# A convolution by blocked transforms, with its inverses taken from the last block to the first, its four-term product summed during the forward transforms, and three gate steps behind the last inverse

## Chip, cores and metric

The kernel runs on one core of one Trainium2 chip. The metric is the device time of one launch in microseconds (us), the median of several runs. One launch computes the forward pass and all gradients.

## The reference, cut to what matters

```python
xn = _layernorm(x)                                  # L=2048 rows, D=576 columns
P  = jnp.exp(logdA[:, :, None] * l)                 # l = 0..L-1, N=128 modes
K  = jnp.einsum("dn,dnl,dn->dl", Cc, P, dB).real    # one kernel of length L per column
y  = irfft(rfft(xn, 2L) * rfft(K, 2L))[:L] + xn * Dskip
h  = _silu(xn @ w1) * (xn @ w3)                     # F=4608
out_0 = x + y * _silu(h @ w2)
out_1..out_12 = gradients of out_0 for the inputs, with grad_out
...
```

What follows the forward pass (the backward of the feed-forward net, of the convolution and of the kernel K) is not touched by the change.

## The kernel before, in words

The program is written as calls with a wished time (`self.at(us)`); a scheduler puts each engine's instructions in an order by these times and by the dependences, and the engines then run their lists strictly in that order, each instruction waiting for its inputs. `issue_after(x)` pins an instruction behind another. DMAs are issued from SP's list or POOL's list, so a DMA that has to wait holds everything behind it in that list.

Three streams of work overlap up to about 620 us:

- **Kernel-making** (`ssm_kernel`, `kgen_chunk`, `kgen_sum`): K is made in 36 chunks of 16 columns. For each chunk ch SP loads the table E_l (L666, issued two chunks ahead in the program), DVE negates one half of it into the other (the negate, L691), PE makes phases (et_ps, L711), ACT turns them into sines (cs_k, L713), DVE makes the products p_k (L719), q_k (L725), t_k (L732) and v_k (L736), and two chunks later PE sums v_k·q_k into kps (L749), which DVE or ACT copies into KT (L757). q_k stays in DRAM for the backward.
- **Gate steps** (`ffn_hidden`): 72 steps, numbered 0 to 71, of two row tiles each. A step is 16 matmuls of 128x512 into pgu (L1076) and 4 of 64 rows (L1084), two s_t (L1088) and two gu_t (L1089) on ACT, one h_t (L1092) on DVE, a store of h_t to H_dram on SP (L1095) and a store of gu_t to GUF_dram on POOL (L1097). `gate_mark` names for each step an earlier matmul of the convolution (`self.marks`) behind which the step's first matmul is pinned; 51 of the steps go with kernel-making, 21 with the convolution.
- **Convolution** (`ssm_conv`, `conv_half`): the columns are done in two halves h of 288, each with NB=4 blocks of 512 rows. Forward: for each block b PE makes the transform of K (L866, 32 matmuls into et_ps), ACT copies it out (kraw, L869, 8 instructions), DVE makes the variants k2, kz (L907 to L909, L959 to L963), and ACT scales kraw by signs (L965) for the next block. The transforms U of xn lie in DRAM. For output block m the product V = sum over i of K_i·U_(m-i) has m+1 terms: the first costs DVE one L917, L923, L925 and L926, a further one also L920 and L921. PE inverts V (L901, 16 matmuls), ACT copies (ev, L990), DVE adds and subtracts (s_t, L992, L993), POOL stores to S_dram (L994). Before the change all four forward blocks of a half come first, then m = 0, 1, 2, 3 with one to four terms, so the longest product stands last.

`ffn_output` then makes h·w2 for 16 row tiles. Slices of h come transposed from H_dram (hcA, hcB, hcC, L1726, on SP), the first 16 groups of w2 lie in w2a, the other 20 in w2g (ten loads on POOL, L1145, each of two groups). Tiles 0 and 1 first take the 32 matmuls with w2a each, then the 40 with w2g (L1170). The S_dram rows of a tile are loaded by POOL as s_t (L1162), x and grad_out as x_t (L1160) and go_t (L1161). Tiles 0 to 3 belong to block m=0.

Of the kernel before, what the change touches and what calls it, by code (L numbers as in the profile page):

```python
# [100 lines left out]
class K:  # L101
# [542 lines left out]
    def ssm_kernel(self, T0, TK, ps, ps1):  # L644
# [8 lines left out]
        with self.pool(name="kg_l", bufs=2) as lp, \  # L653
# [24 lines left out]
            for ch in range(NCH):  # L678
                yield T0 + TK * ch
                self.at(T0 + TK * ch)  # L680
                if ch in (20, 24):
                    self.dft_kernel_matrices(dp, (ch - 20) // 4)
                if ch % GE == 0:
                    LT_ = ahead if ch else load_lhs(0)
                elif ch % GE == 2 and ch + GE < NCH:
                    ahead = load_lhs(ch - 2 + GE)
                for c in range(3) if ch == 0 else (ch + 2,):
                    if c < NCH:
                        load_E(c)
                E, el = Es.pop(ch), self.kg_load  # L690
                nc.vector.tensor_scalar(out=E[:, 0:HW_], in0=E[:, HW_:2 * HW_], scalar1=-1.0, scalar2=None, op0=ALU.mult)  # L691
# [237 lines left out]
    def ssm_conv(self, T0, TC, ps, ps1):  # L929
        with self.pool(name="c_u", bufs=1) as up, \  # L930
# [6 lines left out]
            for h in range(2):  # L937
                self.conv_half(h, T0 + TC * h * 92, TC, kp, up, rp, ypool, tp, spool, epool, ps)

    def conv_half(self, h, T0, TC, kp, up, rp, ypool, tp, spool, epool, ps):  # L940
# [5 lines left out]
        K2, Kz, U = [], [], []  # L946
        prev = None
        fl = lambda t_: t_.rearrange("p q k d -> p q (k d)")
        self.at(T0)
        nc.vector.tensor_tensor(out=self.KT[0:1, 0, cs], in0=self.KT[0:1, 0, cs], in1=self.skip_row[:, cs], op=ALU.add)  # L950
        for b in range(NB):
            self.at(T0 + TC * 4.5 * b)
# [20 lines left out]
            Kz.append(kz)  # L973
            if h == 0 and b == NB - 1:
                with self.tc.issue_after(self.tails[-1].ins):
                    nc.gpsimd.dma_start(out=self.odd["grad_out"][:], in_=self.turned(self.aps["grad_out"].flatten_outer_dims()))
        for m in range(NB):
            self.at(T0 + TC * (18, 28, 43, 65)[m])
            u = up.tile([P, 2, 2, KT, HW], BF16, name=f"u_{m}")
            nc.sync.dma_start(out=u[:].rearrange("p q r k d -> p q (r k d)"),  # L980
                              in_=self.UH_dram[2 * h:2 * h + 2, m].rearrange("q p r k d -> p q (r k d)"))
            U.append(u)
            V = ypool.tile([P, 2, 2, KT, HW], BF16, name="V")
            for i in range(m + 1):
                self.cmul_acc(V, K2[i], Kz[i], U[m - i], tp, i == 0, False)
# [21 lines left out]
    def gate_time(self, n):  # L1007
# [3 lines left out]
        return self.KG[0] + 2 + self.KG[1] * 36 * min(i / self.GK, 1) + 7.0 * max(i - self.GK, 0)  # L1011

    def gate_mark(self, n):
# [3 lines left out]
        h, k = divmod(i - self.GK, 11)  # L1017
        return 36 + 8 * h + ((-1, 0, 1, 1, 2, 3, 3, 4, 5, 5, 6), (-1, 0, 1, 2, 3, 3, 4, 5, 5, 6))[h][k]
# [82 lines left out]
    def ffn_output(self, T0, TB):  # L1101
# [9 lines left out]
        with ExitStack() as es:  # L1111
# [3 lines left out]
            hpc, epc, ip4, gap6, hp, wpool, ipx2 = op("hc"), op("epc"), op("st", 3), op("gap6"), op("h"), op("w"), op("in2x")  # L1115
# [17 lines left out]
            turns = [[(f, f + HB, s0 + f // HB) for f in range(0, FE, HB)] + [(FE, FT, s1)] for (s0, s1) in ((42, 66), (57, 67))]  # L1133
            turns.append([(0, FT // 2, 71), (FT // 2, FT, 71)])
            w2a = self.ktp.tile([P, F0, D], BF16, name="w2a", tag="KT")
            for fi in range(0, FT, GRP):
# [899 lines left out]
def kernel(  # L2036
# [35 lines left out]
    with k.ctx:  # L2072
# [8 lines left out]
        with k.pool(name="xT", bufs=1) as xp, k.pool(name="kg_sel", bufs=1) as selp, \  # L2081
# [6 lines left out]
            k.ssm = k.ssm_forward(*k.KG, 0.83)  # L2088
# [42 lines left out]
```

## Time and profile before

| what | value |
|---|---|
| median of 3 runs (lowest, highest) | 1809.8 us (1797.02, 1814.61) |
| the profiled execution, its span | 1795.53 us, 1793.8 us |
| mean granted TensorE clock | 0.977 |
| busy over the span: PE, DVE, ACT, POOL | 91%, 76%, 50%, 19% |
| PE busy in 100 to 400 us (kernel-making with gate steps) | 274.18 of 300 us |
| PE busy in 550 to 600 us (last inverse, first products with w2) | 18.79 of 50 us |
| DMA share in these two stretches | 0.92, 0.99 |

A row of the timeline has the start, the busy time, the engine, the line, the operation with output and inputs, and how many instructions of that kind the row holds; brackets at its end give the idle time of the engine just ahead of it and what ended that. A row of the waits has the engine and line that waited, what for, the time in total, how often, and the longest. "DMA share" is the mean busy share of the 16 DMA engines, and a sum over overlapping packets, so it can pass 1.

### The profile page before, as it was taken

To read this page: it belongs to the slowest core of one execution; us is meant where nothing else is said; L and a number is where in the kernel's file an instruction comes from. 1 tells how busy PE (TensorE), PEld (TensorE's weight loads), DVE (VectorE), ACT (ScalarE), POOL (GpSimd) and SP (SyncE) were. 2 spreads that over 40 slices of the span, in tenths; PEclk is the share of its full clock that TensorE was granted. 3 is DMA by queue.
4 is the path that set the end of the run, shared out by engine and by line. 5 is a ranking of instruction groups with operands and counts; after the bars stand their busy time and mean duration, and the time that the engine had idled before them with its cause. 6 is when DMAs were issued, how large, how long until landed. Compare 5 with 4: busy or idle time off the path is not lost. (4 is left out here: it accounts for less than half of the span.)

```text
span 1793.8 us, 34839 instructions
## 1 busy us (share of the span) xinstructions
PE 1634.4 (91%) x13765; PEld 1196.3 (67%) x13765; DVE 1359.8 (76%) x2221; ACT 894.0 (50%) x1509; POOL 332.6 (19%) x536
## 2 busy tenths in 40 slices
PE   5889997999994699999999999999999998999997
PEld 2444443445442477788888888888788876778876
DVE  7667767778985355697786978659999974978665
ACT  4778786888672011576765756646454510001001
POOL 3101111111223111111111011111111144131132
PEclk9999999999998799999999999999999999999999
DMA  7879998888789989877587685679999899999991
GB/s 209 274 252 357 328 328 301 295 318 281 247 222 215 187 194 206 231 180 191 173 226 220 183 224 162 184 213 208 254 258 237 208 251 238 235 240 211 212 233 46
DMA packets 632441, 414.02 MB, mean 231 GB/s; under 512 B 427558, under 2 KB 575766, under 8 KB 627670
## 3 DMA queue, kind: packets, MB, share of 16 engines
q1 hardware_dynamic: 585228, 284.79, 64.9%
q0 software_dynamic: 32928, 114.91, 19.8%
q10 hardware_dynamic: 14122, 12.10, 2.5%
q8 instruction: 108, 1.77, 0.4%
q14 instruction: 55, 0.45, 0.1%
HBM read 130.88 MB, written 191.94 MB: 180 GB/s over the span
## 5 line engine op out<-in xcount | busy, mean ns | idle before, releaser
L1076 PE MATMUL pgu<-wmB_w,xnT 128*128 128x512 bf16 x1152 | 281.4, 384 | 5.9 <-ACT gu_t L1089 5.5
L1915 PEld LDWEIGHTS <-acts 128*128 128x128 bf16 x2304 | 225.6, 99 | 62.6 <-DMA acts<-GU_dram 3.3
L1864 PEld LDWEIGHTS <-xn_bf 128*128 128x128 bf16 x2304 | 224.1, 98 | 43.3 <-issue 17.2
L1449 DVE TENSOR_TENSOR pr_q<-et_ps,pz 128x1024 f32<-128x1024 f32 x144 | 175.9, 1222 | 29.1 <-PE et_ps L1444 20.6
L1076 PEld LDWEIGHTS <-xnT 128*128 128x128 bf16 x1152 | 108.5, 99 | 125.0 <-issue 27.2
L1915 PE MATMUL px<-wT,acts 128*128 128x288 bf16 x1472 | 191.1, 288 | 0.0
L1452 DVE TENSOR_REDUCE S_all<-pr_q 128x32 f32<-128x1024 f32 x144 | 175.2, 1217 | 3.2
L1803 PE MATMUL ph<-w2T,goT 128*128 128x256 bf16 x1440 | 172.0, 273 | 3.2 <-ACT gh L1806 3.2
L1803 PEld LDWEIGHTS <-goT 128*128 128x128 bf16 x1440 | 139.1, 98 | 21.6 <-issue 5.6
L1844 PE MATMUL pgw<-go_o,h_n 128*128 128x288 bf16 x1152 | 148.6, 286 | 0.3 <-DVE h_n L1778 0.2
L1089 ACT CAST gu_t<-pgu 128x1024 bf16<-128x1024 f32 x144 | 147.6, 1025 | 0.1
L1864 PE MATMUL pgw<-gu_n,xn_bf 128*128 128x256 bf16 x1152 | 134.5, 272 | 10.0 <-ACT gw L1848 5.9
L1097 POOL DMA_DIRECT2D GUF_dram<-gu_t x72 | 65.3, 907 | 364.4 <-ACT gu_t L1089 348.5
L1864 PE MATMUL pgw<-gg_n,xn_bf 128*128 128x256 bf16 x1152 | 130.4, 272 | 2.2 <-ACT gw L1866 2.0
L1844 PEld LDWEIGHTS <-h_n 128*128 128x128 bf16 x1152 | 112.2, 98 | 29.5 <-issue 1.8
L1088 ACT ACTIVATE s_t<-pgu 128x512 bf16<-128x512 f32 x144 | 87.9, 611 | 77.7 <-PE pgu L1076 48.2
L1866 ACT CAST gw<-pgw 128x256 bf16<-128x256 f32 x144 | 52.3, 374 | 142.0 <-PE pgw L1864 141.9
L1915 PE MATMUL px<-wA,acts 128*128 128x288 bf16 x832 | 110.7, 289 | 4.4 <-DMA acts<-GU_dram 2.7
L1806 ACT CAST gh<-ph 128x512 bf16<-128x512 f32 x144 | 81.2, 600 | 57.8 <-PE ph L1803 54.4
L1982 ACT ACTIVATE go<-gx 128x576 bf16<-128x576 f32 x15 | 10.2, 683 | 193.9 <-DVE gx L1963 146.8
L1849 POOL DMA_DIRECT2D out_dram<-gw x36 | 20.2, 560 | 335.3 <-ACT gw L1848 230.6
L713 ACT ACTIVATE cs_k<-et_ps 128x512 bf16<-128x512 int16 x144 | 75.6, 625 | 0.0
(329 smaller groups left out, 2999.2 us busy)
## 6 DMA issues: line engine op xcount, KB each, us to landing
GUF_dram<-gu_t POOLq DMA_DIRECT2D x72, 512.0 KB, 5.7
H_dram<-h_t SPq DMA_DIRECT2D x72, 256.0 KB, 3.7
Q_dram<-q_k SPq DMA_DIRECT2D x36, 512.0 KB, 4.2
gg_n<-GUF_dram POOLq DMA_DIRECT2D x18, 1024.0 KB, 6.4
h_n<-GUF_dram POOLq DMA_DIRECT2D x18, 1024.0 KB, 8.7
GG_dram<-gg_n SPq DMA_DIRECT2D x36, 512.0 KB, 10.8
GU_dram<-gu_n SPq DMA_DIRECT2D x36, 512.0 KB, 5.1
E_dram<-E_k SPq DMA_DIRECT2D x54, 256.0 KB, 2.3
```

The costliest lines, as they stand in the source:

```text
L713: self.sin_last = nc.scalar.activation(out=CS[:, :, o:o + 256], in_=pt[:].bitcast(I16)[:, :, 0::2], func=ACT.Sin, scale=6.283184 / 2 ** 16)
L1076: ins = nc.tensor.matmul(pt, lhsT=xnT[:, c, ts], rhs=wm[w][:, c, :], start=(q == 0 and c == 0), stop=(q == 1 and c == nfull - 1))
L1088: nc.scalar.activation(out=s_t[:, :, q, :], in_=pg.rearrange("p (g f) -> p g f", g=ng), func=ACT.Silu)
L1089: nc.scalar.copy(out=gu_t[:, :, :, q, :], in_=pgu[:].rearrange("p k (g f) -> p k g f", g=ng))
L1097: self.u_stores[step] = nc.gpsimd.dma_start(out=self.GUF_dram[fb * ng:(fb + 1) * ng, :, :, i0:i0 + NT, :].rearrange("g p k t f -> p k g (t ...
L1449: nc.vector.tensor_tensor(out=pr[:].rearrange("p r k e -> p r (k e)"), in0=T[x][:].rearrange("p k z d a -> p (k z d a)")[:, None].to_broad ...
L1452: nc.vector.tensor_reduce(out=self.S_all[:, :, d0:d0 + 4], in_=pr[:].rearrange("p r k (d a) -> p (r k) d a", d=4), op=ALU.add, axis=AX.X)
L1803: self.pe_last = nc.tensor.matmul(ph[j][:, k, :].rearrange("p (a f) -> p a f", f=P), lhsT=lw, rhs=rh, start=(n == 0), stop=(n == nfull))
L1806: self.sc(lambda: nc.scalar.copy(out=gh[:, j], in_=ph[j][:]))
L1844: self.pe_last = nc.tensor.matmul(pgw[pi_][:, 0:pw], lhsT=hn[:, tt, fl * P:(fl + 1) * P], rhs=go_o[:, tt, po:po + pw], start=(tt == 0), st ...
L1864: self.pe_last = nc.tensor.matmul(pw_[:, 0:FG], lhsT=self.xn_bf[:, tt, c * P:(c + 1) * P], rhs=nat[:, tt, :], start=(tt == 0), stop=(tt == ...
L1915: self.pe_last = nc.tensor.matmul(px[pi_][:, 0:pw], lhsT=acts[i][:, ai, fi, :], rhs=w[:, po:po + pw], start=(n == 0), stop=(n == len(steps ...
```

## The change

Five edits go together.

- The negate of chunk ch is pinned behind the last v_k made (that of chunk ch-1).
- In `conv_half` all four U loads move ahead of the forward blocks; V of the last block (m=3) is summed one product per forward block; the inverses then run m = 3, 2, 1, 0 with new wished times; the forward blocks have a wished distance of 8 in place of 4.5, and the second half starts at 70 in place of 92 (in units TC, now 1 and no more 0.83).
- Gate steps behind kernel-making have a wished distance of 7.4 (was 7.0) and a new table of marks: one mark for each step, so that steps 69, 70 and 71 stand behind the last inverse.
- In `ffn_output` the transposes of H (`turns`) are pinned behind later steps, and two pools change places.
- The w2g loads are pinned behind the GUF stores of steps 69 to 71, where they were pinned behind those of steps 61 to 70.

```diff
@@ ssm_kernel
-                nc.vector.tensor_scalar(out=E[:, 0:HW_], in0=E[:, HW_:2 * HW_], scalar1=-1.0, scalar2=None, op0=ALU.mult)
+                with self.tc.issue_after(self.v_last.ins) if ch else nullcontext():
+                    nc.vector.tensor_scalar(out=E[:, 0:HW_], in0=E[:, HW_:2 * HW_], scalar1=-1.0, scalar2=None, op0=ALU.mult)
@@ ssm_conv
-                self.conv_half(h, T0 + TC * h * 92, TC, kp, up, rp, ypool, tp, spool, epool, ps)
+                self.conv_half(h, T0 + TC * h * 70, TC, kp, up, rp, ypool, tp, spool, epool, ps)
@@ conv_half
+        self.at(T0 - 10)
+        for m in range(NB - 1, -1, -1):
+            U[m] = up.tile([P, 2, 2, KT, HW], BF16, name=f"u_{m}")
+            nc.sync.dma_start(out=U[m][:].rearrange("p q r k d -> p q (r k d)"),
+                              in_=self.UH_dram[2 * h:2 * h + 2, m].rearrange("q p r k d -> p q (r k d)"))
...
-            self.at(T0 + TC * 4.5 * b)
+            self.at(T0 + TC * 8 * b)
...
+            if b == 0:
+                V = ypool.tile([P, 2, 2, KT, HW], BF16, name="V")
+            self.cmul_acc(V, k2, kz, U[NB - 1 - b], tp, b == 0, False)
...
-        for m in range(NB):
-            self.at(T0 + TC * (18, 28, 43, 65)[m])
-            u = up.tile([P, 2, 2, KT, HW], BF16, name=f"u_{m}")
-            nc.sync.dma_start(out=u[:].rearrange("p q r k d -> p q (r k d)"),
-                              in_=self.UH_dram[2 * h:2 * h + 2, m].rearrange("q p r k d -> p q (r k d)"))
-            U.append(u)
-            V = ypool.tile([P, 2, 2, KT, HW], BF16, name="V")
-            for i in range(m + 1):
-                self.cmul_acc(V, K2[i], Kz[i], U[m - i], tp, i == 0, False)
+        for m in range(NB - 1, -1, -1):
+            self.at(T0 + TC * (64, 56, 48, 36)[m])
+            if m < NB - 1:
+                V = ypool.tile([P, 2, 2, KT, HW], BF16, name="V")
+                for i in range(m + 1):
+                    self.cmul_acc(V, K2[i], Kz[i], U[m - i], tp, i == 0, False)
@@ ffn_output
-                        with self.tc.issue_after(self.u_stores[61 + (fi - F0 + j) // 2].ins):
+                        with self.tc.issue_after(self.u_stores[69 + (fi - F0 + 4) // 12].ins):
```

**DVE in kernel-making**, at chunk 21. The number behind a name tells the tile: E_l_3239 is the table from which q_k_3454 and p_k_3455 are made, E_l_3434 and E_l_3558 are those of chunks 23 and 24. Before:

```order
L691 TENSOR_SCALAR E_l_3434<-E_l_3434 128x512
L691 TENSOR_SCALAR E_l_3558<-E_l_3558 128x512
L725 TENSOR_TENSOR q_k_3454<-cs_k_3437,E_l_3239 128x2x16x32 x2
L719 TENSOR_TENSOR p_k_3455<-cs_k_3437,E_l_3239 128x2x4x128
L732 TENSOR_TENSOR t_k_3461<-p_k_3455,WT_1157 128x1024 x2
L736 TENSOR_TENSOR v_k_3464<-t_k_3461 128x1024
```

and with the change:

```order
L737 TENSOR_TENSOR v_k_3379<-t_k_3376 128x1024
L1098 TENSOR_TENSOR h_t_3404<-s_t_3403,gu_t_3402 128x2x2x256
L692 TENSOR_SCALAR E_l_3239<-E_l_3239 128x512
L758 CAST KT_1296<-kps_3466 64x16x8 x2
L726 TENSOR_TENSOR q_k_3454<-cs_k_3437,E_l_3239 128x2x16x32 x2
L720 TENSOR_TENSOR p_k_3455<-cs_k_3437,E_l_3239 128x2x4x128
L733 TENSOR_TENSOR t_k_3461<-p_k_3455,WT_1157 128x1024 x2
```

Before, the negates of chunks 23 and 24 stand ahead of this chunk's q_k, and its own negate stood 30 rows earlier, some two chunks ahead. With the change its own negate stands right behind the v_k of the chunk before and two rows ahead of its q_k, and no table of a later chunk is touched ahead of it.

**ACT in the second half's forward blocks** (kraw is the copied transform, s_t and gu_t the gate steps' instructions). Before:

```order
L965 ACTIVATE kraw<-kraw,sgn 128x2304
L1088 ACTIVATE s_t<-pgu 128x2x256
L1089 CAST gu_t<-pgu 128x4x256
L1088 ACTIVATE s_t<-pgu 128x2x256
L1089 CAST gu_t<-pgu 128x4x256
L869 ACTIVATE kraw<-et_ps,hrowM 128x2x144 x2
L869 ACTIVATE kraw<-et_ps 128x2x144 x6
L965 ACTIVATE kraw<-kraw,sgn 128x2304
L869 ACTIVATE kraw<-et_ps,hrowM 128x2x144 x2
L869 ACTIVATE kraw<-et_ps 128x2x144
L1088 ACTIVATE s_t<-pgu 128x2x256
L869 ACTIVATE kraw<-et_ps 128x2x144 x2
```

and with the change:

```order
L971 ACTIVATE kraw<-kraw,sgn 128x2304
L1094 ACTIVATE s_t<-pgu 128x2x256
L1095 CAST gu_t<-pgu 128x4x256
L1094 ACTIVATE s_t<-pgu 128x2x256
L1095 CAST gu_t<-pgu 128x4x256
L870 ACTIVATE kraw<-et_ps,hrowM 128x2x144 x2
L870 ACTIVATE kraw<-et_ps 128x2x144 x6
L971 ACTIVATE kraw<-kraw,sgn 128x2304
L1094 ACTIVATE s_t<-pgu 128x2x256
```

Before, the copies of the third block are mixed with the gate step's instructions, and the sign scaling is followed by the next block's copies at once. With the change every block has the sign scaling, then a whole gate step, then the eight copies of the next block.

**POOL behind the last inverse** (s_t_6705, s_t_6754 and s_t_6911 are the S_dram rows of tiles 0, 1 and 2). Before:

```order
L1162 DMA s_t_6754<-S_dram 128x576
L994 DMA S_dram<-s_t 128x2x288
L1160 DMA x_t<-in_A_u_dram 128x576
L994 DMA S_dram<-s_t 128x2x288
L1161 DMA go_t<-in_grad_out_dram 128x576
L1160 DMA x_t<-in_A_u_dram 128x576
L1161 DMA go_t<-in_grad_out_dram 128x576
L1162 DMA s_t_6911<-S_dram 128x576
L1145 DMA w2g_6678<-in_B_w_dram 128x2x576 x2
L1145 DMA w2g_6681<-in_B_w_dram 128x2x576 x2
L1145 DMA w2g_6684<-in_B_w_dram 128x2x576 x2
L1145 DMA w2g_6687<-in_B_w_dram 128x2x576 x2
```

and with the change:

```order
L1000 DMA S_dram<-s_t 128x2x288 x2
L1167 DMA x_t<-in_A_u_dram 128x576
L1169 DMA s_t_6705<-S_dram 128x576
L1169 DMA s_t_6754<-S_dram 128x576
L1169 DMA s_t_6911<-S_dram 128x576
L1103 DMA GUF_dram<-gu_t 256x2x512
L1152 DMA w2g_6678<-in_B_w_dram 128x2x576 x2
L1152 DMA w2g_6681<-in_B_w_dram 128x2x576 x2
L1103 DMA GUF_dram<-gu_t 256x2x512
L1152 DMA w2g_6684<-in_B_w_dram 128x2x576 x2
L1152 DMA w2g_6687<-in_B_w_dram 128x2x576 x2
```

Before, the rows of tiles 0 and 1 are loaded ahead of the last two S_dram stores, and the ten w2g loads follow together. With the change the loads for all three tiles stand behind the last stores, the first four w2g loads behind the GUF store of step 69, and the other six behind that of step 70; the store of step 71 (not shown) follows them.

More of the change, by code (lines that the diff above doesn't have):

```diff
@@ L1010, in gate_time @@
         i = n - self.LEAD
-        return self.KG[0] + 2 + self.KG[1] * 36 * min(i / self.GK, 1) + 7.0 * max(i - self.GK, 0)
+        return self.KG[0] + 2 + self.KG[1] * 36 * min(i / self.GK, 1) + 7.4 * max(i - self.GK, 0)
     def gate_mark(self, n):
@@ L1016, in gate_mark @@
             return i * 36 // self.GK - 1
[L1017 to L1018 removed]
+        i -= self.GK
+        return 35 + i if i < 5 else 36 + (4, 4, 5, 6, 7, 8, 9, 10, 11, 12, 12, 13, 14, 15, 15, 15)[i - 5]
     def ffn_hidden(self, wp, gup):
```

13 lines of the change are left out of this document (7 added, 6 removed).

## The prediction

> **What bounds the kernel now.** I read the busy shares first, then a table by stage, then the waits of the two stages that the change touches, then the timeline at the longest idle times of PE. The table's columns are the stretch, its length, busy time of PE, weight loads, DVE, ACT and POOL, the granted clock, the DMA share and GB/s.
>
> ```profile
> PE 1634.4 (91%) x13765; PEld 1196.3 (67%) x13765; DVE 1359.8 (76%) x2221; ACT 894.0 (50%) x1509; POOL 332.6 (19%) x536
> 100.00:400.00 300.00, 274.18 (x1879) 132.23 (x1879) 218.18 (x423) 237.34 (x399) 47.41 (x53) 0.97 0.92 313
> 411.40:566.40 155.00, 130.21 (x771) 66.73 (x770) 133.61 (x185) 101.14 (x162) 36.02 (x44) 0.96 0.81 243
> 620.00:700.00 80.00, 79.80 (x647) 62.65 (x648) 46.15 (x68) 11.13 (x24) 13.25 (x25) 0.98 0.81 192
> ```
>
> PE is the bound, and from 620 us on it has hardly an idle moment (79.80 of 80), so what the program gains or loses before then passes through to the end. Ahead of it two stages leave PE idle: 25.8 us in kernel-making (300 - 274.18), 24.8 us in the convolution (155 - 130.21), where DVE is as busy as PE. A row of the waits of 90 to 406 us:
>
> ```profile
> DVE E_l L691 <- DMA E_l<-E_dram: 52.5, 24, 6.5
> ```
>
> DVE stood 24 times at the negate for a table that had not landed, up to 6.5 us. At the end of the convolution the waits name other causes, whose rows stand further down: PE stood 15 us for the longest product and then twice for w2g.
>
> **The change part by part.** *The negate.* Five of these waits reach PE. First the three longest of them on DVE, then the rows of PE behind all five, with the eight matmuls at 302.74 as a measure:
>
> ```profile
> 266.58 0.29 DVE L691 TENSOR_SCALAR E_l<-E_l 128x512 bf16<-128x512 bf16 x1 [6.48 <-DMA E_l<-E_dram]
> 307.37 0.29 DVE L691 TENSOR_SCALAR E_l<-E_l 128x512 bf16<-128x512 bf16 x1 [6.22 <-DMA E_l<-E_dram]
> 366.10 0.29 DVE L691 TENSOR_SCALAR E_l<-E_l 128x512 bf16<-128x512 bf16 x1 [5.02 <-DMA E_l<-E_dram]
> ...
> 198.84 0.63 PE L749 MATMUL kps<-v_k,q_k 128*128 128x64 bf16 x16 [2.86 <-DVE KT L757]
> 270.40 0.63 PE L749 MATMUL kps<-v_k,q_k 128*128 128x64 bf16 x16 [2.11 <-DVE KT L757]
> 270.86 2.95 PE L1076 MATMUL pgu<-wmB_w,xnT 128*128 128x512 bf16 x8
> 302.74 1.89 PE L1076 MATMUL pgu<-wmB_w,xnT 128*128 128x512 bf16 x8
> 313.17 0.58 PE L711 MATMUL et_ps<-SEL,lhs_t 128*128 128x256 bf16 x2 [5.62 <-ACT cs_k L713]
> 313.55 3.06 PE L1076 MATMUL pgu<-wmB_w,xnT 128*128 128x512 bf16 x8
> 332.62 0.75 PE L749 MATMUL kps<-v_k,q_k 128*128 128x64 bf16 x16 [2.04 <-DVE KT L757]
> 333.84 2.71 PE L1076 MATMUL pgu<-wmB_w,xnT 128*128 128x512 bf16 x6
> 367.36 0.63 PE L749 MATMUL kps<-v_k,q_k 128*128 128x64 bf16 x16 [1.06 <-DVE KT L757]
> ```
>
> The gaps sum to 2.86 + 2.11 + 5.62 + 2.04 + 1.06 = 13.7 us. Behind three of them the next matmuls run slowly: eight take 2.95 and 3.06 where eight take 1.89 elsewhere, and six take 2.71 where 1.42 (six eighths of 1.89) would do, together 1.06 + 1.17 + 1.29 = 3.5 us. So 17.2 us is the upper bound of these five. The Trainium skill's page "TensorE: Matmul & The Clock Gate", Part 1, says that the array falls to half its clock only after an idle window of about 3.4 us; by that rule only the gap of 5.62 would bring slow matmuls, and the bound would be 13.7 + 1.2 = 14.9. The trace does not bear it out that strictly: eight matmuls took 2.95 us behind a gap of 2.11.
>
> Will the wait be gone? The order shows the negate of a chunk behind the v_k of the chunk before, two or so chunks later than it stood. A load lands within 9.2 us of its issue:
>
> ```profile
> DMA to landing us min/median/max: 3.3/5.1/9.2
> ...
> L691 DVE TENSOR_SCALAR E_l<-E_l x36: 284/294/295, 109.3 to 380.2; 128x512 bf16<-128x512 bf16 x36
> ```
>
> The negates from 109.3 to 380.2 give a chunk each 7.7 us (271 / 35), so two chunks are 15 us of cover, more than the longest landing; SP's list has the loads where they were. What the negate costs itself (0.29) does not change. What is late next? The other small waits (25.8 - 13.7 = 12.1 us) stay, and the DMA share of 0.92 would rise to 0.97 if the stage shrank by 15 us. I take 15 of the 17.2, and for the range 3 (if most of it turns into other waits) to 19 (if small idle times go too).
>
> *The convolution's own work* is the same: 20 products, 8 transforms, 8 inverses; only the order moves. The rows for DVE (busy, mean ns), the first transform and its scaling, two products in a row, and three sign scalings of the second half:
>
> ```profile
> L921 DVE TENSOR_TENSOR V<-V,cm_t 128x2304 bf16<-128x2304 bf16 x12 | 16.1, 1343 | 0.0
> L925 DVE TENSOR_TENSOR V<-V,cm_t 128x1152 bf16<-128x1152 bf16 x20 | 14.9, 747 | 0.1
> ...
> 406.43 0.65 PE L866 MATMUL et_ps<-KT,dC 128*128 128x288 bf16 x4
> 414.15 2.22 ACT L965 ACTIVATE kraw<-kraw,sgn 128x2304 bf16<-128x2304 bf16 x1
> ...
> 486.80 2.21 ACT L965 ACTIVATE kraw<-kraw,sgn 128x2304 bf16<-128x2304 bf16 x1 [0.90 <-DVE kz L960]
> ...
> 487.21 1.28 DVE L917 TENSOR_TENSOR V<-k,u 128x2304 bf16<-128x2304 bf16 x1
> 488.42 1.33 DVE L923 TENSOR_TENSOR cm_t<-u,kz 128x2304 bf16<-128x2304 bf16 x1
> ...
> 496.63 2.22 ACT L965 ACTIVATE kraw<-kraw,sgn 128x2304 bf16<-128x2304 bf16 x1 [1.31 <-DVE kz L963]
> 504.19 2.23 ACT L965 ACTIVATE kraw<-kraw,sgn 128x2304 bf16<-128x2304 bf16 x1
> ...
> L1092 DVE TENSOR_TENSOR h_t<-s_t,gu_t 128x1024 bf16<-128x1024 bf16 x22 | 15.0, 680 | 13.8 <-DMA H_dram<-h_t 13.5
> L992 DVE TENSOR_TENSOR s_t<-ev,et_ps 128x288 bf16<-128x288 f32 x16 | 7.0, 438 | 2.5 <-ACT ev L990 2.2 <-issue 0.2
> ```
>
> A first term is two full instructions (like L921) and two halves (like L925), 2 x 1.34 + 2 x 0.75 = 4.2 us; a further term is three full ones and two halves, 5.5. Instructions overlap by some 0.1 each (488.42 starts 1.21 behind 487.21, which takes 1.28), so I use 3.9 and 5.2. The new order chains, on ACT, the sign scaling, a whole gate step and the copies of the next block. The one block that went so before took 496.63 - 486.80 = 9.8 us, the mixed one 504.19 - 496.63 = 7.6. A half is then: first scaling 7.7 us after its first transform matmul (414.15 - 406.43), three times 9.8, and 7 for the last block's variants and term; then the products with three, two and one terms, 3 x 3.9 + 3 x 5.2 = 27, with four h_t (0.7) and eight additions (0.44) some 6 more in all. First half: 406.4 + 7.7 + 29.4 + 7 + 33 = 483.5. The second half's first transforms stand on PE behind the last inverse (2.2) and a gate step (16 matmuls at 302.74's rate and their tails, 4.2), so its first scaling comes at 483.5 + 14 = 497.5, and the chain ends at 497.5 + 29.4 + 7 + 33 = 567, the inverse at 569. Before, the last inverse ended at 565.80 + 3.42 = 569.2 (row below). So the stage ends where it did, with DVE waiting some 2.6 us in each block (9.8 less 7.2 of variants, term and h_t) in place of 13.5 us for H_dram. Bounds: a pitch of 7.6 makes it 6 x 2.2 = 13 earlier, 11 makes it 7 later.
>
> *Three gate steps behind the last inverse and the w2g loads.* Rows of before:
>
> ```profile
> 565.80 3.42 PE L901 MATMUL et_ps<-V,cT 128*128 128x288 bf16 x16 [15.03 <-DVE V L925]
> 570.44 0.72 POOL L994 DMA_DIRECT2D S_dram<-s_t  x1
> 572.98 4.08 PE L1170 MATMUL po<-w2a,hcB 128*128 128x288 bf16 x32
> 579.97 5.63 POOL L1145 DMA_DIRECT2D w2g<-in_B_w_dram  x8 [3.98 <-DMA x_t<-in_A_u_dram]
> 582.73 2.08 PE L1170 MATMUL po<-w2g,hcA 128*128 128x288 bf16 x8 [5.66 <-DMA w2g<-in_B_w_dram]
> 595.32 5.78 PE L1170 MATMUL po<-w2g,hcA 128*128 128x288 bf16 x28 [10.52 <-DMA w2g<-in_B_w_dram]
> 601.81 5.06 PE L1170 MATMUL po<-w2g,hcB 128*128 128x288 bf16 x40
> w2g<-in_B_w_dram POOLq DMA_DIRECT2D x10, 288.0 KB, 15.7
> S_dram<-s_t POOLq DMA_DIRECT2D x16, 144.0 KB, 4.9
> ```
>
> PE gets three steps of 4.2 that stood earlier before, and the two w2a blocks of 4.08 as before: 569 + 12.6 + 8.2 = 590 for the first w2g product. On POOL the last S_dram store is issued at about 570, and the three s_t loads behind it need it landed, 4.9 us by the median: 575; then the first four w2g loads, and the last six behind the store of step 70, near 583, held as before by older POOL DMAs (3.98) and issued over some 4 us: 587 to 590. With 15.7 us to landing the last arrive at 603 to 606, and 5.7 us of products follow (0.65 of tile 0, 5.06 of tile 1): 608 to 611, against 606.87 before. If the loads land in half that time because the ring is emptier, PE alone sets the end: 590 + 10.5 = 600. So this part is worth -7 to +5; I take 0. The page "DMA: Bandwidth & Descriptors", section "Anatomy of one DMA", of the Trainium skill has about 2.0 us fixed and bytes over 436 GB/s, by which 288 KB would land in 2.7 us and the end would be the 600; the measured 15.7, at a DMA share near 1, says that here the queue and not the transfer sets it.
>
> **Sum:** -15 + 0 + 0 = -15 against the profiled execution of 1795.5 (span 1793.8 and 1.7 around it): 1780.5. The median of the runs shown is 1809.8, 0.8% above that execution, so the forecast in its terms is 1794.8.
>
> **The rivals.** *(a) The convolution gains too.* If ACT's chain runs at 7.6 a block, since the gate step's copies no longer wait behind DVE, the last inverse comes 13 us earlier and w2g with it: -28, 1781.8. For it: DVE has 155 - 133.6 = 21 us to spare there, and the three steps cover w2g's landing. Against it: the chain of copies is in ACT's list now, word by word.
>
> *(b) Slower: the blocks wait for PE as well.* ACT's list has a gate step between scaling and copies; if that step's matmuls stand on PE behind the block's transform and are not done when ACT comes, a block takes 9.8 + 4.2 = 14.0. Six such intervals cost 25: -15 + 25 = +10, 1820. It decides from a pitch of 12.3 us on (6 x 2.5 = 15). For it: PE's marks now pin one step to each block. Against it: PE holds two pgu buffers, so a step can run ahead.
>
> *(c) The negate's wait only moves.* If the load is late because the DMA engines are full, q_k waits where the negate did: kernel-making gains 3, 1807. For it: DMA share 0.92. Against it: the wait was for tables two to three chunks ahead of their use.
>
> **How the numbers follow.** Forecast 0.47 (1794.8, its own range 1785 to 1802), (a) 0.20, (b) 0.14, (c) 0.19. The range of 8 in 10 reaches from below (a) to between (c) and (b): 1771 to 1815. A measurement of this kernel tells about 1% (18 us) from no change. Faster by more needs -18: nearly all of (a), and four in ten of the forecast's, 0.39. Slower by more needs +18, the upper part of (b) and the spread of the runs: 0.11. The same: 0.50.
>
> **What would show it.** Right: no wait of the negate for E_l beyond a few us, 52.5 before; PE busy some 274 of 285 where it was 300; the first transform near 391 in place of 406; sign scalings 9.8 apart; last inverse ending 163 us after the first transform, as before; first w2g product waiting less than 5.66 and 10.52, and the last of tile 1 200 us after the first transform. Wrong: a new wait of q_k for E_l or of PE for cs_k with 10 us or more; scalings over 12 apart; a stage behind 620 that gets longer.

## The result and the profile after

| | before | changed |
|---|---|---|
| median (lowest to highest, 20 runs each) | 1807.78 us (1787.31 to 1830.5) | 1790.7 us (1779.1 to 1807.54) |
| ratio to before, 95% interval | | 0.9932 (0.9904 to 0.996) |
| span of the profiled execution, granted clock | 1793.8 us, 0.977 | 1777.3 us, 0.983 |

The kernel became faster by 0.7%, some 12 us (0.0068 x 1807.78), where 15 were forecast; the ratio rests on the undisturbed runs, so it is a little nearer to 1 than that of the medians. In the changed file all lines stand a few further down: the negate is L692, the transforms L867, the inverses L902, the sign scaling L971, the products with w2 L1177, the transposes of h L1733.

Four landmarks on PE split the time: the first forward transform, the end of the last inverse, the end of row tile 1's products with w2, and the start of tile 4's. The second figure is the distance from the first transform.

| landmark | before | changed |
|---|---|---|
| first transform starts | 406.43 | 385.96 |
| last inverse ends | 569.2 (162.8) | 554.8 (168.8) |
| tile 1's products end | 606.87 (200.4) | 589.64 (203.7) |
| tile 4's products start | 630.94 (224.5) | 617.45 (231.5) |
| rest of the span behind that | 1162.9 | 1159.9 |

The start of tile 4's products in the old kernel, and in the changed one the end of the last inverse, of tile 1's products and the start of tile 4's (that row is cut off by the end of its view):

```profile
630.94 4.08 PE L1170 MATMUL po<-w2a,hcB 128*128 128x288 bf16 x32
```

```profile
554.13 0.65 PE L902 MATMUL et_ps<-V,cT 128*128 128x288 bf16 x4 [0.42 <-ACT ev L996]
...
584.58 5.06 PE L1177 MATMUL po<-w2g,hcB 128*128 128x288 bf16 x40
...
617.45 2.74 PE L1177 MATMUL po<-w2a,hcB 128*128 128x288 bf16 x21
```

In these two profiles kernel-making gave 20.5 us, and the convolution with the first row tiles took 7.0 of them back. The stage table of the old kernel, from 100 us to the first transform and from there to the end of tile 1's products (columns as in the prediction):

```profile
100.00:406.43 306.43, 280.47 (x1927) 135.36 (x1926) 222.72 (x432) 242.35 (x408) 48.32 (x54) 0.97 0.92 313
406.43:606.87 200.44, 159.24 (x968) 87.55 (x967) 143.33 (x204) 108.12 (x175) 49.35 (x66) 0.92 0.89 237
```

and of the changed one:

```profile
100.00:385.96 285.96, 272.64 (x1926) 132.30 (x1926) 224.20 (x433) 241.63 (x408) 48.35 (x54) 0.99 0.97 336
385.96:589.64 203.68, 167.70 (x967) 90.53 (x966) 141.55 (x200) 109.17 (x175) 48.55 (x64) 0.92 0.73 217
```

In the first stage PE's idle time fell from 26.0 to 13.3 us (length less busy) and its busy time, for the same 1926 matmuls, from 280.5 to 272.6: 12.6 us of waiting and 7.8 of slower matmuls are gone. In the second the idle time fell too, from 41.2 to 36.0, but the same matmuls took 8.5 us longer.

The waits of the convolution and of the first row tiles in the changed kernel (engine and line, what for, total, times, longest):

```profile
PE et_ps L902 <- DVE V L926: 23.6, 6, 6.2
...
PE et_ps L867 <- ACT kraw L870: 7.3, 7, 2.0
...
PE po L1177 <- DMA hcA<-H_dram: 6.1, 1, 6.1
```

and from its timeline on PE the first transform, the inverses that waited, and the first products with w2g:

```profile
385.96 0.65 PE L867 MATMUL et_ps<-KT,dC 128*128 128x288 bf16 x4
...
430.60 2.97 PE L902 MATMUL et_ps<-V,cT 128*128 128x288 bf16 x16 [1.98 <-DVE V L926]
448.68 4.00 PE L902 MATMUL et_ps<-V,cT 128*128 128x288 bf16 x16 [5.90 <-DVE V L926]
460.06 3.45 PE L902 MATMUL et_ps<-V,cT 128*128 128x288 bf16 x16 [3.29 <-DVE V L926]
...
514.67 3.45 PE L902 MATMUL et_ps<-V,cT 128*128 128x288 bf16 x16 [3.28 <-DVE V L926]
532.51 4.00 PE L902 MATMUL et_ps<-V,cT 128*128 128x288 bf16 x16 [6.20 <-DVE V L926]
544.33 3.70 PE L902 MATMUL et_ps<-V,cT 128*128 128x288 bf16 x16 [2.99 <-DVE V L926]
...
574.75 2.12 PE L1177 MATMUL po<-w2g,hcA 128*128 128x288 bf16 x16
578.95 0.65 PE L1177 MATMUL po<-w2g,hcA 128*128 128x288 bf16 x4 [2.08 <-DMA w2g<-in_B_w_dram]
...
606.77 5.44 PE L1177 MATMUL po<-w2a,hcA 128*128 128x288 bf16 x32 [6.12 <-DMA hcA<-H_dram]
```

Where PE waited four times for a product, 18.9 us in all and 15.03 of it for the longest, it now waits six times, 2.0 to 6.2 us each and 23.6 in all, and each of the six waits is followed by slow matmuls: the 16 of such an inverse take 3.0 to 4.0 us, while twelve inverse matmuls that did not wait took 1.63 (467.44 in this timeline), so 16 take 2.2. The granted clock was 0.50 in the slow stretch from 448.70 to 452.50 and 1.00 from 467.44 to 469.00. The w2g waits shrank from 16.2 to 4.0 us in total. What is new is the wait for tile 3's transpose, 6.12 where it was 3.60.

### The profile page after: what moved, and what is told of

Read it like the earlier page. It is cut to its first block, busy times and chain, and to the rows that moved or that the text cites. A ratio compares the mean times of both kernels' runs of the same rounds, so it can differ in the third digit from the quotient of the medians.

```text
span 1777.3 us, 34850 instructions
## 1 busy us (share of the span) xinstructions
PE 1632.5 (92%) x13765; PEld 1195.1 (67%) x13765; DVE 1361.8 (77%) x2221; ACT 893.2 (50%) x1509; POOL 332.9 (19%) x536
## 5 line engine op out<-in xcount | busy, mean ns | idle before, releaser
L1098 DVE TENSOR_TENSOR h_t<-s_t,gu_t 128x1024 bf16<-128x1024 bf16 x72 | 49.6, 689 | 59.3 <-ACT gu_t L1095 57.5
```

## The experiments

Theory A: the moved negate brings the whole gain and more, by taking a wait out of DVE's list; the other edits together cost a few microseconds. Rival R: the convolution's new order brings a good part. Beside the ratios (to the old kernel, same chip, 95% interval) stand the landmarks of one profiled execution each. The rest of the span behind tile 4's start ran from 1159.6 to 1168.6 us over the profiles whose code there is alike, so that a span alone tells differences of under 9 us badly. The landmarks spread less, but they spread too: e3 and e10 below are the same kernel, and their first transforms start at 389.16 and 385.43, tile 4's products 217.0 and 223.3 us behind that. A difference of a few microseconds between two profiles is no more than a hint.

### The negate alone, and all the rest alone

```diff
# e1: the kernel before, with the negate's pin only
+                with self.tc.issue_after(self.v_last.ins) if ch else nullcontext():
+                    nc.vector.tensor_scalar(out=E[:, 0:HW_], in0=E[:, HW_:2 * HW_], scalar1=-1.0, scalar2=None, op0=ALU.mult)
# e2: the changed kernel, without the negate's pin
-                with self.tc.issue_after(self.v_last.ins) if ch else nullcontext():
-                    nc.vector.tensor_scalar(...)
+                nc.vector.tensor_scalar(...)
```

> The kernel before with only the negate of the table E_l pinned behind the v_k of the chunk before; convolution, gate marks, transposes and w2g loads as before. Theory A (the moved negate brings more than the whole gain, the other edits give a few us back): no wait of DVE for E_l, the first transform starts near 386 us instead of 406 (as in the changed kernel), and this kernel ends 17 to 21 us before the old one, ratio 0.988 to 0.991, some 3 to 7 us faster than the changed kernel. Rival R (the convolution's new order brings a good part): 8 to 12 us faster than before, ratio 0.993 to 0.996, slower than the changed kernel.

> The changed kernel with the negate put back to where it was; all other edits stay. Theory A: the first transform is back near 406 us, DVE waits some 50 us for E_l again, and the kernel is 2 to 7 us slower than before, ratio 1.001 to 1.004. Rival R: 3 to 8 us faster than before, ratio 0.996 to 0.998.

Measured: e1 0.9894 (0.985 to 0.9937), span 1778.4; e2 1.0043 (1.0009 to 1.0078), span 1812.9. First transform and start of tile 4's products in e1:

```profile
384.63 0.65 PE L867 MATMUL et_ps<-KT,dC 128*128 128x288 bf16 x4
...
611.42 4.08 PE L1171 MATMUL po<-w2a,hcB 128*128 128x288 bf16 x32
```

and in e2, with the wait of DVE that is back (waits of 90 to 406 us):

```profile
405.98 0.65 PE L866 MATMUL et_ps<-KT,dC 128*128 128x288 bf16 x4
...
645.75 4.08 PE L1176 MATMUL po<-w2a,hcB 128*128 128x288 bf16 x32
```

```profile
DVE E_l L691 <- DMA E_l<-E_dram: 53.4, 24, 6.0
```

Theory A holds and R falls: the negate alone moves the first transform by 21.8 us, and the other edits alone make the kernel slower than before, with an interval clear of 1 (tile 4 starts 239.8 us after the first transform, before 224.5). The product of both ratios, 0.9894 x 1.0043 = 0.9937, is the changed kernel's 0.9932 within the errors. That the negate alone beats the changed kernel is likely by these numbers but not settled by this run: the intervals overlap. One thing in e1 was not foreseen: its convolution stage is longer than before, though its order is the old one. The last inverse ends 170.5 us after the first transform (162.8 before, 168.8 in the changed kernel), and tile 4 starts at 226.8 (before 224.5), with DVE waiting 19.7 us for H_dram instead of 13.5.

### The negate on POOL

```diff
-                nc.vector.tensor_scalar(out=E[:, 0:HW_], ...)
+                nc.gpsimd.tensor_scalar(out=E[:, 0:HW_], ...)
```

> The kernel before with the negate of E_l done by POOL instead of DVE, at the same wished place; nothing else changed. The wait for the table's load is still there, but now POOL stands in it. Theory A (DVE standing in its list for a table needed two or three chunks later is what delayed PE): DVE no longer waits, the first transform starts at 384 to 390 us, as with the pinned negate. Rival (the pin helped by giving DVE another order, or the tables themselves are late for q_k): the first transform stays beyond 398 us, and q_k waits for POOL's negate.

> The kernel before with the negate on POOL, the same kernel as in the earlier look, now timed in five rounds since its two runs were the fastest so far. Theory A (it takes the same stall off DVE as the pin does): ratio 0.986 to 0.991, like the pinned negate alone (0.9894). If freeing DVE of the negate brings more than the pin: 0.980 to 0.985.

Measured: 0.9821 (0.9735 to 0.9908) for e3, over two runs, and 0.9877 (0.9833 to 0.992) for e10, over six; first transform at 389.16 and 385.43. The wait did not go away, it changed engines (the group in e3, then the waits in e10):

```profile
L691 POOL TENSOR_SCALAR E_l<-E_l 128x512 bf16<-128x512 bf16 x36 | 58.9, 1638 | 142.8 <-DMA E_l<-E_dram 115.7 <-DVE h_t L1092 10.3 <-DVE p_k L719 7.4
```

```profile
POOL E_l L691 <- DMA E_l<-E_dram: 108.4, 23, 26.0
```

POOL stands 108 us for the tables, twice what DVE did, and takes 1.6 to 1.7 us for each negate instead of 0.29, and still the first transform comes as early as with the pin. So neither the table's lateness nor DVE's own work was the cost, but DVE's standing in its list with q_k, v_k and the copies to KT queued behind. This bears out theory A against its rival, by a way that keeps the negate at its old wished place. The ratio of e10 lies within what was expected for "the same as the pin".

### The stalls put back

```diff
+                for _ in range({12: 2, 21: 4, 26: 4, 28: 1, 33: 3}.get(ch, 0)):     # e12: {12: 5, 17: 5, 22: 5, 27: 5, 32: 5}
+                    with self.tc.issue_after(stall.ins):
+                        stall = nc.vector.scalar_tensor_tensor(out=E[:, HW_:], in0=E[:, HW_:], scalar=1.0, in1=E[:, HW_:], op0=ALU.mult, op1=ALU.max)
```

> The changed kernel with five stalls of DVE put back by work instead of by DMA: behind the v_k of chunks 11, 20, 25, 27 and 32 DVE multiplies the table by one, 2, 4, 4, 1 and 3 times, some 1.6 us each, 22 us in all, about what the five waits lasted that reached PE in the kernel before. The output does not change. Theory A (these stalls, and the slow matmuls behind the gaps that they make, are the 20 us): the first transform moves from 386 to 396 to 406 us, with gaps of 1 to 5 us on PE and matmuls above 0.3 us behind them. Rival (DVE has slack of 70 us there, and it was the loads' DMA traffic that slowed PE): the first transform stays below 391 us.

> The changed kernel with five equal stalls of DVE by work: ahead of the negates of chunks 12, 17, 22, 27 and 32 DVE multiplies the table by one five times, 1.75 us each, 8.8 us a stall and 44 us in all. The output does not change. The earlier kernel with stalls of up to 7 us left gaps of at most 1.7 us on PE and no slow matmuls behind them; in the kernel before, gaps of 2.0 to 5.6 us were each followed by eight matmuls or so that took 1.1 to 1.2 us too long. Theory A (a gap of about 2 us or more is enough for slow matmuls, about 1.2 us for each gap whatever its length): gaps of 2 to 4 us, 1.0 to 1.3 us of slow matmuls behind each of at least three of them, first transform at 402 to 412 us. Rival (only gaps above 3.4 us are followed by slow matmuls, and what was slow in the kernel before was slow for another reason, such as DMA traffic): no slow matmuls behind the gaps of 2 to 3.4 us.

Measured: e6 0.9965 (0.9925 to 1.0004), first transform at 396.94, 11.0 us later than in the changed kernel for 14 x 1.75 = 24.5 us of added DVE work. e12 1.0007 (0.9947 to 1.0067), first transform at 405.70, 19.7 later for 25 x 1.75 = 43.8 us. By its ratio the whole gain of the change is lost in e12. The exchange is the same as for the old wait: 11.0 / 24.5 = 0.45, 19.7 / 43.8 = 0.45, and in the old kernel 20.5 / 52.5 = 0.39. So time that DVE loses in that stage, in pieces of some 1.75 us or more, moves PE, whether DVE works or waits in it; the loads were those of the changed kernel, so no other DMA traffic is needed for it. The 36 x 0.29 us that e10 takes off DVE, in single small pieces, moved nothing beyond the pin. The second half of the expectations failed: the added work, cut up by one other instruction between each two, made PE wait often and briefly (nothing over 1.74 in e6, 1.6 behind the added work in e12), not in gaps of 2 to 4 us, so e12 did not try what it was made for. It has one slow stretch, quoted in the last section.

### The convolution without its tail, and with the negate on POOL

```diff
# e9: the kernel before, with the pin, the new ssm_conv and conv_half, and TC = 1
#     (gate_time, gate_mark, turns, pools and w2g pins as before)
# e11: the changed kernel
-                with self.tc.issue_after(self.v_last.ins) if ch else nullcontext():
-                    nc.vector.tensor_scalar(out=E[:, 0:HW_], ...)
+                nc.gpsimd.tensor_scalar(out=E[:, 0:HW_], ...)
```

> The kernel before with the pinned negate and the new convolution (products summed during the forward transforms, inverses from last to first), but with the old gate marks, transposes and w2g pins: only half a gate step stands behind the last inverse. The changed kernel starts tile 4's products 231.5 us after the first transform, the old one 224.5. Theory C (the new order of the convolution costs these 7 us, the three gate steps behind it win some back by covering w2g): tile 4 starts 232 us or more after the first transform, PE waits over 8 us for w2g, and the kernel is as fast as the changed one or slower, ratio to the old kernel 0.992 to 0.998. Theory T (the tail costs them: the gate steps, transposes and w2g loads moved late): tile 4 starts at 226 us or earlier, and the kernel is 4 to 8 us faster than the changed one, ratio 0.987 to 0.991.

> The changed kernel with its negate on POOL at the old wished place instead of pinned on DVE. Theory A (the other edits cost 4 to 10 us whatever frees DVE): slower than the old kernel with the negate on POOL by 4 to 10 us, ratio to the old kernel 0.989 to 0.995. Rival (the new order pays off once kernel-making is free of the stall by another way): as fast as the old kernel with the negate on POOL or faster, 0.980 to 0.988.

These two and the timed e10 ran on the same chip and share the runs of the kernel before: e10 0.9877 (0.9833 to 0.992), e9 0.9964 (0.9939 to 0.9989), e11 0.996 (0.9929 to 0.9991). All three start the first transform between 385 and 388 us. The pair e11 and e10, whose intervals do not touch, prices the other four edits together, with the negate on POOL in both: some 0.8%, 15 us. In their profiles it is 18.8 us by the start of tile 4 (242.1 less 223.3 from the first transform), but only 2.4 of these lie ahead of the end of the last inverse (169.1 less 166.7). Behind it e11 has the three gate steps, and PE still waits 13.7 us for w2g, where e10 without these steps waits 15.2; so there the steps hide next to nothing of that wait. The start of tile 4's products in e10, then in e11 with that wait:

```profile
608.73 4.08 PE L1170 MATMUL po<-w2a,hcB 128*128 128x288 bf16 x32
```

```profile
627.64 4.08 PE L1176 MATMUL po<-w2a,hcB 128*128 128x288 bf16 x32
```

```profile
PE po L1176 <- DMA w2g<-in_B_w_dram: 13.7, 3, 7.3
```

The pair e9 and e1 prices the new convolution alone, with the pin and the old tail in both: 0.9964 against 0.9894 (0.985 to 0.9937, on another chip), some 0.7%, with intervals that just miss each other. Their two profiles do not show where it goes: the last inverse ends 170.7 us after the first transform in e9 and 170.5 in e1, and tile 4 starts at 228.6 and 226.8. So theory C is borne out by the times as far as the cost of the new convolution goes; its two other numbers were missed: tile 4 started 228.6 us after the first transform in e9, between both expectations, and PE waited 6.5 us for w2g, not over 8. What the three gate steps behind the last inverse are worth by themselves is not resolved: e9's interval overlaps the changed kernel's.

### Three tries at the convolution's cost

```diff
# e4: transposes of tiles 4 and 5 behind tile 3's
-                    with self.tc.issue_after(self.h_stores[step].ins) if step else nullcontext():
+                    with self.tc.issue_after(self.h_stores[step].ins if step else self.hc_loads[3].ins) if step or i in (4, 5) else nullcontext():
# e5: second half earlier
-                self.conv_half(h, T0 + TC * h * 70, TC, ...)
+                self.conv_half(h, T0 + TC * h * 60, TC, ...)
# e7: both first late gate steps behind the first block (e8: e5 and e7 together)
-        return 35 + i if i < 5 else 36 + ...
+        return (36, 36, 37, 38, 39)[i] if i < 5 else 36 + ...
```

> The changed kernel with the transposes of row tiles 4 and 5 of h pinned on SP behind that of tile 3. In the changed kernel PE waits 6.1 us for tile 3's transpose, which was issued 12 us after its buffer came free, behind tile 4's. Theory A (SP's order makes that wait): the wait shrinks to under 2 us and the kernel is 4 to 6 us faster than the changed one, ratio to the old kernel 0.989 to 0.991. Rival (the transposes are slow in total, so tile 4 is late instead): the wait moves to tile 4 and the time stays that of the changed kernel, ratio 0.992 to 0.995.

Measured: 0.9918 (0.9885 to 0.9951), not to be told from the changed kernel. The wait for hcA is gone, and another one stands 10 us further on (PE, e4):

```profile
604.21 4.08 PE L1177 MATMUL po<-w2a,hcA 128*128 128x288 bf16 x32
614.18 0.64 PE L1237 MATMUL ptr<-ident_bf,go_o 128*128 128x128 bf16 x5 [4.42 <-DVE go_o L1194]
619.71 2.49 PE L1177 MATMUL po<-w2a,hcB 128*128 128x288 bf16 x19
```

Behind it stands SP's list, and then DVE:

```profile
600.04 6.20 SPq L1733 DMA_TRANSPOSE hcB<-H_dram  x1
606.34 0.53 SPq L1197 DMA_DIRECT2D GS_dram<-gs_t  x1
...
611.35 0.76 DVE L1196 TENSOR_TENSOR gs_t<-go_t,g 128x576 bf16<-128x576 bf16 x1 [4.66 <-DMA GS_dram<-gs_t]
```

The store of gs_t now stands behind the transpose of tile 4, DVE needs its buffer back, and PE needs what DVE makes after. The rival is right that the wait moves, though to a store and not to tile 4's transpose: SP's list is full there.

> The changed kernel with the second half of the convolution wished at 60 instead of 70: its first two forward transforms stand right behind the last inverse of the first half, ahead of a gate step. In the changed kernel DVE is idle for some 11 us between the halves. Theory A (the convolution is bound by the chain of DVE and ACT, and the gap between the halves is on it): the last inverse ends 4 to 8 us earlier after the first transform than the changed kernel's 168.7 us, and the whole is 3 to 7 us faster than the changed kernel. Rival (PE or the w2g loads set the end of this stage): the last inverse is earlier but the last product of row tile 1 is not, and the time stays within 2 us of the changed kernel.

> The changed kernel with the first two of its 21 late gate steps both pinned behind the first forward block, so that ACT copies that block's transform at once; in the changed kernel a gate step stands inside the block and its first sign scaling comes 13.9 us after the first transform instead of 7.7. Theory A (the chain of blocks sets the convolution's end): the first scaling comes 7 to 9 us after the first transform, the last inverse ends 162 to 165 us after it instead of 168.7, and the kernel is 3 to 6 us faster than the changed one. Rival (the time given back early is lost again at the products, where DVE is full, or at the w2g loads): the last inverse comes at 167 us or later, and the time stays within 2 us of the changed kernel.

> The edit of the first block and the second half wished at 60 instead of 70, together, on the changed kernel. If both act on the same chain and add up: 5 to 10 us faster than the changed kernel, ratio to the old kernel 0.987 to 0.990, at least as fast as the negate alone. If the w2g loads or PE set the stage's end: no faster than each edit alone.

Measured: e5 0.9895 (0.986 to 0.993), e7 0.9884 (0.9833 to 0.9935), e8 0.9882 (0.9827 to 0.9937). All three ratios lie below the changed kernel's, by 0.004 to 0.005, but their intervals overlap its own, and the landmarks do not show a gain of that size: the last inverse ends 165.5, 168.5 and 166.8 us after the first transform (changed 168.8), tile 1's products 201.9, 202.8 and 199.7 (203.7), and tile 4 starts at 234.3, 231.1 and 234.2 (231.5). The last inverse of e5 comes 3.3 us earlier, short of the 4 to 8 that theory A expected, and that of e8 lies between those of e5 and e7, so the two edits do not add up there. Whether they are faster stays open. All three have the new order and stand level with e1 (0.9894) by their ratios, so the cost found for the new order may lie in its marks and wished times; no run here separates that. What e7 shows is where its time went, in the sign scalings:

```profile
392.96 2.21 ACT L971 ACTIVATE kraw<-kraw,sgn 128x2304 bf16<-128x2304 bf16 x1 [0.90 <-DVE kz L966]
405.32 2.21 ACT L971 ACTIVATE kraw<-kraw,sgn 128x2304 bf16<-128x2304 bf16 x1 [3.51 <-DVE kz L969]
414.83 2.22 ACT L971 ACTIVATE kraw<-kraw,sgn 128x2304 bf16<-128x2304 bf16 x1
```

The first comes 7.25 us after the first transform, as planned, but the second 12.4 later, since the gate step that was moved out of the first block now stands in the second. The third comes 29.1 us after the first transform, in the changed kernel 29.7. Moving the step does not shorten the chain. The last inverse, at 168.5, is where the rival put it, though the time went to the second block and not to the products or to w2g; whether the run time stays within the rival's 2 us the ratios do not tell.

## Why the prediction was right, point by point

**The negate (forecast -15, bound 17.2; measured -20.5).** The mechanism holds (e1, e2, e3 and e10), and so does the sum of the gaps: 13.7 us were counted, 12.6 of PE's idle time went. What was mis-sized is the term of slow matmuls, 3.5 us in the forecast, 7.8 measured as less busy time for the same matmuls, so 17.2 was no bound. I had counted three slow groups, taken from the first row behind three of the gaps, and had called the sum an upper bound. The old trace has more of them; behind the gap at 198.84, for which I had counted none (old kernel):

```profile
199.30 3.06 PE L1076 MATMUL pgu<-wmB_w,xnT 128*128 128x512 bf16 x8
202.16 1.37 PE L711 MATMUL et_ps<-SEL,lhs_t 128*128 128x256 bf16 x6
```

The eight take 1.17 too long, and six of the phases 1.37 where 0.82 is their usual time (as at 380.23 in the changed kernel). In the changed trace no group of gate-step matmuls of that stage is slow like these. Then I took 15 of the 17.2 for new waits that might come; none came. PE's largest waits there are now 2.5 us for gu_t and 2.4 for cs_k in total.

**The rival "the wait only moves" (c)** is refuted: q_k waits for no table, although the DMA share did rise to 0.97 as worked out.

**The convolution (forecast 0: last inverse 162.6 us after the first transform, as before; measured 168.8).** "As before" was itself an unsteady measure: with DVE freed, the old order ends at 170.5 (e1), 166.7 (e10) and 165.1 (e3), so these 6 us cannot be put down to the new order. The chain's terms, forecast and measured in the changed trace:

| term | forecast | measured |
|---|---|---|
| first transform to first scaling | 7.7 | 13.9 (385.96 to 399.84) |
| two further scalings, first half | 19.6 | 15.8 (to 415.64) |
| last block and its term, to the first inverse | 16.8 | 15.0 (to 430.60) |
| products with three, two and one terms | 33 | 36.8 (to 467.44) |
| to the second half's first scaling | 14 | 12.8 (to 480.19) |
| two further scalings | 19.6 | 19.0 (to 499.23) |
| last block | 16.8 | 15.4 (to 514.67) |
| products | 33 | 37.4 (to 552.08) |
| last inverse | 2 | 2.7 |

The pitch of the blocks, on which the forecast rested most, was right in the second half (9.5, forecast 9.8). In the first half it was 7.9, near the 7.6 of rival (a), but the first block took 6.2 us more than forecast. The over 12 of rival (b) did not come, and neither did the earlier end of (a). Two terms were too small: the first block has a whole gate step inside it, which the order shows and I had not looked at there; and the products took 4 us more a half than 3.9 and 5.2 a term plus h_t and additions. e7 shows that the first cannot be saved by moving the step, since the next block takes it instead. Of the second the first half's trace shows the parts: the last product is done 2.2 us late (465.76), since DVE made twelve additions and not eight and waited some 1.5 us, and its inverse then stands 1.7 behind a gate step on PE until 467.44.

**The tail (forecast 0, tile 1's products ending 608 to 611, which is 202 to 205 from the first transform; measured 203.7).** This came out, but for other reasons in part. PE reached the w2g products 188.8 us after the first transform (forecast 590, 183.6), and most of the loads were there: 4.0 us of waiting instead of 16.2. The 15.7 us to landing, from which the forecast took its late end, were too long for these loads, which took 9.3 by the median. That this is not safe e11 shows, where the same tail left 13.7 us of waiting.

**What the forecast left out** is the row behind that: SP's list of transposes. Tile 3's buffer came free when tile 0's products ended at 584.6, but its transpose was issued at 596.50, behind those of tiles 2 and 4 (SP, changed kernel):

```profile
586.00 4.03 SPq L1733 DMA_TRANSPOSE hcC<-H_dram  x1
590.40 6.00 SPq L1733 DMA_TRANSPOSE hcB<-H_dram  x1
596.50 6.53 SPq L1733 DMA_TRANSPOSE hcA<-H_dram  x1
```

The stretch from tile 1's end to tile 4's start is 3.7 of the 7.0 us (203.7 to 231.5 against 200.4 to 224.5); 2.5 of it is this wait, 6.12 against 3.60. I had read SP's list up to the last H_dram store and not to the third tile.

**The sum.** -20.5 + 7.0 = -13.5 by tile 4's start, and -12 by the runs, against -15: two errors of opposite sign, 5.5 in kernel-making and 7 behind it. The total was right by luck, since its two errors nearly cancelled; its split was not. The old convolution with a freed DVE is some 7 us better than the changed kernel by e1's ratio (0.9894 against 0.9932, intervals overlapping) and 15 by e10 against e11.

**What stays open.** Where the other four edits lose their time is not settled. At the start of tile 4's products the four profiles with the old order lie 217.0 to 226.8 us behind the first transform, the ten with the new one 228.6 to 242.1. At the end of the last inverse they overlap: 162.8 to 170.5 and 165.5 to 170.7. In these profiles the cost is clear only behind the last inverse, and there e9 (228.6), with the new order and the old tail, lies too near e1 (226.8) to part the order from the tail. Slow matmuls are one candidate: PE's idle time from the first transform to tile 1's end is smaller in the changed kernel (36.0 against 41.2), and its busy time larger by 8.5 us for the same matmuls; six of the slow groups are inverses that had waited, 21.6 us in all where 13.2 would do at 2.2 each. Whether those 8.5 us delay the end, or lie in time in which PE would have waited for DVE anyway, no run here separates: none kept the waits and took away the slowness.

## What to carry to other kernels

A small instruction that needs a late load can cost not its own time but that of all that is queued behind it on its engine; look for a wait whose result is needed much later than it is made, and put the instruction next to its use or on an engine with nothing to delay (here 20 us for 36 instructions of 0.29 us). Where the bounding engine waits in several short pieces, look for slow work behind each gap: in the old kernel the gate-step matmuls lost 1.1 to 1.3 us more behind each of four gaps of 2.0 to 5.6 us, and over the stage the slow work came to some 0.6 of what the gaps themselves were worth (7.8 against 12.6). When a change has an independent part, time that part alone: the kernel with the lowest ratio here, that of e3 and e10, moves only the negate, though the interval of e10 overlaps those of e1, e5, e7 and e8.

## What the runs showed of the hardware

Slow matmuls do not need one long gap. In the old kernel gaps of 2.11 and 2.86 us were followed by eight matmuls in 2.95 and 3.06 instead of 1.89, and one of 2.04 by six in 2.71 instead of 1.42, with a granted clock of 0.60 from 199.30 to 202.10 and of 1.00 at the usual eight of 302.74. In e12 seven took 3.10 (443 ns each, 236 usual) behind a stretch with two gaps of 1.00 and 0.44 and small matmuls in between, with a granted clock of 0.54 from 320.56 to 323.66 (PE, e12):

```profile
316.75 0.39 PE L1094 MATMUL pgu<-wtail,xnT 64*128 64x512 bf16 x1
318.15 0.63 PE L754 MATMUL kps<-v_k,q_k 128*128 128x64 bf16 x16 [1.00 <-DVE KT L762]
318.70 0.39 PE L1094 MATMUL pgu<-wtail,xnT 64*128 64x512 bf16 x1
319.53 0.39 PE L1094 MATMUL pgu<-wtail,xnT 64*128 64x512 bf16 x2 [0.44 <-ACT gu_t L1099]
319.86 0.48 PE L1086 MATMUL pgu<-wmB_w,xnT 128*128 128x512 bf16 x1
320.13 0.63 PE L716 MATMUL et_ps<-SEL,lhs_t 128*128 128x256 bf16 x2
320.56 3.10 PE L1086 MATMUL pgu<-wmB_w,xnT 128*128 128x512 bf16 x7
```

The page "TensorE: Matmul & The Clock Gate" of the Trainium skill, Part 1, describes a free-running activity window of about 3.4 us and an idle window as the condition. Ahead of 320.56 PE was idle for 1.44 of 3.4 us, in two pieces, and in the old kernel for 2.0 to 2.9, so a wholly idle window is not needed here. But single gaps of up to 1.7 us in e6 had no slow matmuls behind them, and neither had one of 2.58 us in e2:

```profile
324.83 1.89 PE L1081 MATMUL pgu<-wmB_w,xnT 128*128 128x512 bf16 x8 [2.58 <-ACT gu_t L1094]
```

So the length of the last gap alone does not decide it, and what does these runs don't tell. Full DMA engines are not needed for it: the DMA share was 0.36 in the slow stretch of the changed kernel from 448.70 to 452.50.

A transpose that SP issued while the w2g loads of POOL were under way took two to three times as long to issue as one behind them: 13.34 us for half of tile 2's (571.99 in the changed kernel, w2g loads issued from 562.83 to 575.2), 15.43 for tile 4's in the old one (575.48), against 4.03 for a half and 4.5 to 6.5 for a whole one behind the loads in the changed kernel; in the old one the first behind them still took 9.24 (604.76). That they share something is only argued from the overlap.
